# A fused retention and SwiGLU kernel: the first head pair by 128 tokens, and the loads of its start in another order

## The chip, the cores and the metric

The kernel runs on one core of a Trainium2 chip. A core has five engines that run at the same time, each through its own instructions in order: TensorE (matmuls; the profile shows weight loads apart from the streaming), VectorE, ScalarE, GpSimd and SyncE. SyncE and ScalarE also issue most of the DMA transfers here, and GpSimd a few. TensorE writes to PSUM, in eight banks; VectorE and ScalarE take results out of there into SBUF.

The metric is the time of one execution on the device, in microseconds (us). A profile of one execution is the source of everything that is said of single instructions.

## The reference

Two stages are fused: a retention (attention with a decay in place of the softmax), and a SwiGLU feed-forward block on its output.

```python
B, H, S, D = 8, 8, 576, 64            # q, k, v, float32
gamma = 1.0 - 2.0 ** (-5.0 - arange(H))
scores = (1 / sqrt(D)) * q @ k.T
ret = scores * where(i >= j, gamma ** (i - j), 0)
attn = ret @ v
x = attn.transpose(0, 2, 1, 3).reshape(4608, 512)
g, val = x @ w_gate, x @ w_val        # 512 x 1536 each, float64
out = (g * sigmoid(g) * val) @ w_out  # 1536 x 512, float64
```

The weights come as float64 and are turned into float32 on the chip.

## The kernel before

**Retention.** The work goes by pairs of heads: pair `i` holds heads `2p` and `2p + 1` of one batch entry, four pairs to an entry, 32 in all. The first four pairs (`i < HP`, HP = 4) make the first 512 tokens of `x`, the first tile; everything below concerns them. A pair is cut into chunks of 64 tokens. In a chunk the decayed scores times the values give its own part ("own values"); what comes from earlier chunks goes through a running state of 64 x 64 per head ("earlier values").

For one pair of the first four the steps are:

- `load(i)` (L254) asks for q, k and v. Pairs 0 and 1 are asked for on SyncE's and ScalarE's queues, one head on each, pairs 2 and 3 on SyncE's. A small table of decays, `tab`, comes first on SyncE's queue (L311); its rest, which the pairs after the first four use, comes between pairs 2 and 3 (L337).
- `scale_run(i)` (L730), GpSimd: the queries of pairs 1 to 3 are multiplied by their decay.
- `transposes(i)` (L448): four 128 x 128 transposes each of k and q on TensorE, copies of the two out of PSUM (`kT` and `qT`; ScalarE, and for pair 0 partly VectorE), and the keys scaled by decay (`keys`, on VectorE for pair 0, ScalarE for pair 1, GpSimd for 2 and 3).
- `scores(i)` and `new_states(i)` (L562, L537): 64 x 64 matmuls into the banks `inner`.
- `masked(i)` (L576): ScalarE copies the even chunks' states (`even`), VectorE multiplies the scores by the decay (`own`), then adds up the states (`pairs`, `odd`, three steps of 64 columns, and `evens`).
- `own_values(i)` and `earlier_values(i)` (L524, L546): 64 x 64 matmuls into the banks `outer`.
- `to_x(i)` (L613): the result goes to the tile of `x`, on VectorE for pair 0, on ScalarE for pairs 1 to 3.

A float32 matmul of the code stands as two records in the trace, a transpose as one: `scores(i)` has 16 matmuls and 32 records.

**Weights.** There are 18 blocks of 1 MB, each for 256 columns of the gate or value weights, or 256 rows of the output weights. `load_w(m)` (L359) asks for the m-th of them, up to `m = 4` on SyncE's queue and later ones on ScalarE's. It writes into one of a few places in turn, so it has to wait for the splits that read the block there before. A block has two halves (128 columns); `halves` numbers them j: 0 is the first half of the first gate block, 1 the first half of the first value block, 2 and 3 their second halves, 4 and 5 the halves of the second gate block, and so on. `split(j)` (L380) is two ScalarE instructions that take the float64 apart, `rounding(j)` (L399) two on VectorE that make the float32; `rounding(j)` also emits `split(j + 1)` unless told not to. `split(2)` emits `load_w(4)`, and `split(3)` puts `load_w(5)` off to a given place.

**Feed-forward of the first tile.** `up0(f, chunks)` (L842) multiplies columns `f` of the gate (into bankA or bankC) and of the value weights (into bankB or bankE) with the given pairs' parts of `x`, one 512-wide matmul for a pair and a weight. It takes banks A and B for even `f`, C and E for odd. When the last pair is in, ScalarE applies the SiLU and VectorE multiplies.

**Order.** From L1425 on each engine's instructions stand in the order in which the code emits them. L1427 to L1436 run the first four pairs: `tick(t, 0, HP)` (L737) has stage by stage one pair's transposes, the next older one's scores and states, and the next older one's values. In `tick(3)` and `tick(4)` the first splits, roundings and `up0(0, [0, 1])`, `up0(1, [0, 1])` stand between; after them come chunks 2 and 3 of both. `load(HP)`, the fifth pair, is issued after `tick(3)`. From L1444 a plan goes on with `up0(2)` to `up0(11)`, the roundings that each needs, and the ticks of pairs 4 to 9; `tick(HP)`, the transposes of pair 4, is its second entry. The tiles after the first (from L1511) take most of the time and are the same before and after.

Of the kernel before, what the change touches and what calls it, by code (L numbers as in the profile page):

```python
# [17 lines left out]
ALU = mybir.AluOpType  # L18
# [4 lines left out]
def tables(gamma, scale, L):  # L23
# [15 lines left out]
             both(g[:, None] ** L), both(g[:, None] ** (2 * L)), pieces, runs, both(scale * g[:, None] ** at),  # L39
# [92 lines left out]
def kernel(  # L132
# [32 lines left out]
    nc = tc.nc  # L165
# [88 lines left out]
    def load(i):  # L254
# [6 lines left out]
        if i < HP:  # L261
# [11 lines left out]
            for h in heads:  # L273
                queues[i % 2].dma_start(out=blocks(t)[:, h % 2], in_=v[b, h, 0:CW].rearrange("(c p) d -> p c d", p=P))
# [35 lines left out]
    NCOL = 6 * H + 4 * HP  # L310
    nc.sync.dma_start(out=tab[:, 0:NCOL], in_=decays[:, 0:NCOL])  # L311
    load(0)
    load(1)
    ident = const.tile([P, P], F32, name="ident")
    make_identity(nc, ident)
    nc.scalar.activation(out=io[:, 0:1], in_=ident[:, 0:1], func=AF.Silu)
    inv, key = tab[:, 0:H], tab[:, H : 2 * H]
    step = tab[:, 2 * H : 2 * H + 2 * HP]
    piece = tab[:, 2 * H + 2 * HP : 2 * H + 4 * HP]
    run = tab[:, 2 * H + 4 * HP : NCOL]  # L320
# [11 lines left out]
    even_heads, odd_heads = slice(0, H, 2), slice(1, H, 2)  # L332
    for rows in half:
        decay(slice(0, H), slice(0, H), rows)

    load(2)
    nc.sync.dma_start(out=tab[:, NCOL:], in_=decays[:, NCOL:])  # L337
    load(3)
# [20 lines left out]
    def load_w(m, parts=range(2)):  # L359

        i, queue = order[m], nc.sync if m < 5 else nc.scalar
# [49 lines left out]
    for f in range(2):  # L411
        for m in range(2):
            load_w(m, (f,))
# [30 lines left out]
    def vector(i):  # L444

        return i == 0

    def transposes(i):  # L448
# [6 lines left out]
        copy = nc.scalar.copy if i else nc.vector.tensor_copy  # L455
        if i < HP:

            mine = (bankC, bankE) if i + 1 == HP else (bankB, bankA)
            parts = [(kT, kn, mine[0]), (qT, qk, mine[1])]
            if i == 0:  # L460
                parts.reverse()

            def turn(t, src, bank):
                for c in range(NFULL):
                    to = bank[:, c : 4 * P : NFULL] if t is qT and scaled(i) else bank[:, ts(c, P)]
                    nc.tensor.transpose(to, src[:, ts(c, P)], ident)

            def put(t, _, bank):
                if i or t is qT:
                    copy(t[:, 0:CW], bank)  # L470
                else:
                    copy(t[:, 0 : CW // 2], bank[:, 0 : CW // 2])
                    nc.scalar.copy(t[:, CW // 2 : CW], bank[:, CW // 2 :])

            if i + 1 == HP:
                for part in parts:
                    turn(*part)
# [1092 lines left out]
```

## Time and profile before

| | |
|---|---|
| median of 3 runs | 1015.25 us (1015.02 to 1017.70) |
| the profiled execution | 1014.55 us, of which 1012.8 us is the span from first to last instruction |
| TensorE streaming | 1000.9 us, 99% of the span |
| TensorE loading weights | 825.5 us, beside the streaming |
| VectorE, ScalarE, GpSimd | 710.9, 286.7, 561.8 us |
| TensorE busy in the first 10 us, in 10 to 20, 20 to 30, 30 to 40 | 4.50, 9.03, 8.83, 9.82 us |
| TensorE busy from 40 to 100 us | 60.00 us |
| data moved in the first 60 us | 15.58 MB |

A view of the profile names an instruction by the line of the code (L532), the engine, the operation, and the tile it writes and reads; `rest` and `arena` are large areas of SBUF that hold many things in turn, `bankA` to `bankE`, `inner` and `outer` are PSUM. "PE" is TensorE, "PEld" its weight loads, "DVE" VectorE, "ACT" ScalarE, "POOL" GpSimd, "SP" SyncE; a q after the name is the engine's sequencer, which issues transfers. "x32" says that 32 such instructions are merged in a row. "[1.16 <-PE outer L559]" says that the engine was idle for 1.16 us before, and what ended that. Busy time of an engine that is not on the chain of waits costs nothing by itself.

### The profile page before, as it was taken

The numbers are of one execution on the slowest core, as the hardware profiler recorded it, in microseconds if no ns is written. First come the engines' busy times: TensorE is split into PE (matmuls) and PEld (weight loads), VectorE is DVE, ScalarE is ACT, GpSimd is POOL, SyncE is SP. The second block draws the span as 40 slices with busy tenths as digits, with TensorE's granted clock in tenths as the row PEclk, the third lists the DMA queues.
The fourth block names the chain that finished last, engine by engine and source line by source line (L and its number), as shares of the span: only waits on it lengthen the run. The fifth ranks groups of instructions, "written<-read, shape, count | busy, mean of one in ns | idle before, by whom it ended". The sixth has DMA issues, their size and how long they took to land.

```text
span 1012.8 us, 21319 instructions
## 1 busy us (share of the span) xinstructions
PE 1000.9 (99%) x8336; PEld 825.5 (82%) x8336; DVE 710.9 (70%) x1206; ACT 286.7 (28%) x636; POOL 561.8 (55%) x589
## 2 busy tenths in 40 slices
PE   6999999999999999999999999999999999999998
PEld 5655555888888888888888888888888888888887
DVE  4488887677875766977777678866575767566645
ACT  4565522132423312133422202233220012232110
POOL 3400359979375228575564157746672586566514
PEclk9999999999999999999999999999999999999999
DMA  9999866967587787647677777434454554445553
GB/s 245 261 288 272 192 216 234 264 193 214 138 238 207 217 231 193 198 156 196 184 202 206 198 179 217 154 133 159 161 172 141 154 189 147 148 155 180 182 159 102
DMA packets 278892, 194.38 MB, mean 192 GB/s; under 512 B 212552, under 2 KB 246088, under 8 KB 278792
## 3 DMA queue, kind: packets, MB, share of 16 engines
q1 hardware_dynamic: 251464, 94.70, 36.7%
q10 hardware_dynamic: 26688, 97.92, 29.1%
q8 instruction: 66, 1.08, 0.5%
q0 software_dynamic: 640, 0.39, 0.2%
q14 instruction: 34, 0.28, 0.1%
HBM read 154.04 MB, written 38.93 MB: 191 GB/s over the span
## 4 chain that ended last, share of the span: by engine, by line
PE 94%; DVE 2%; DMA 1%; POOL 1%; SPq 0%; issue 0%; ACT 0%; DVEq 0%; ACTq 0%; POOLq 0%
PE bankB L1186 12%; PE bankC L1186 11%; PE bankA L1186 11%; PE bankE L1186 11%; PE bankB L1392 7%; PE bankC L1392 7%; PE bankE L1392 6%; PE bankA L1392 6%; PE outer L532 2%; PE bankE L853 2%; PE bankA L853 2%; PE outer L1186 2%; PE inner L1186 2%; PE bankB L853 2%; PE outer L559 2%; PE bankC L853 2%
## 5 line engine op out<-in xcount | busy, mean ns | idle before, releaser
L1042 POOL TENSOR_TENSOR rest<-rest 128x512 f32<-128x512 f32 (+1 forms) x139 | 148.0, 1076 | 159.9 <-DVE rest L1042 112.5
L1201 POOL TENSOR_TENSOR arena<-rest,io 128x256 f32<-128x256 f32 x168 | 123.9, 750 | 89.4 <-ACT io L1200 88.9
L1200 ACT ACTIVATE io<-rest 128x256 f32<-128x256 f32 x192 | 79.3, 417 | 200.0 <-DVE rest L1042 140.0
L1186 PE MATMUL bankB<-rest,arena 128*128 128x256 f32 x448 | 114.5, 380 | 0.0
L1042 DVE TENSOR_TENSOR rest<-bankB,rest 128x512 f32<-128x512 f32 x116 | 78.5, 685 | 40.5 <-PE bankB L1186 28.5
L1186 PE MATMUL bankC<-rest,arena 128*128 128x256 f32 x416 | 106.3, 380 | 0.0
L1186 PE MATMUL bankA<-rest,arena 128*128 128x256 f32 x412 | 104.8, 379 | 0.0
L1042 DVE TENSOR_TENSOR rest<-bankA,rest 128x512 f32<-128x512 f32 x111 | 75.2, 685 | 40.8 <-PE bankA L1186 19.3
L1042 DVE TENSOR_TENSOR rest<-bankC,rest 128x512 f32<-128x512 f32 x110 | 74.5, 683 | 38.0 <-PE bankC L1186 23.4
L1042 DVE TENSOR_TENSOR rest<-bankE,rest 128x512 f32<-128x512 f32 x106 | 71.7, 684 | 36.2 <-PE bankE L1186 17.6
L1186 PE MATMUL bankE<-rest,arena 128*128 128x256 f32 x372 | 94.9, 380 | 0.3 <-DVE rest L1042 0.3
L1186 PEld LDWEIGHTS bankB<-rest,arena 128*128 128x128 f32 x448 | 84.7, 190 | 11.9 <-DVE rest L1042 0.2
L1186 PEld LDWEIGHTS bankC<-rest,arena 128*128 128x128 f32 x416 | 78.5, 190 | 11.4 <-DVE rest L1042 0.8
L1186 PEld LDWEIGHTS bankA<-rest,arena 128*128 128x128 f32 x412 | 78.1, 190 | 10.9 <-DVE rest L1042 0.2
L1186 PEld LDWEIGHTS bankE<-rest,arena 128*128 128x128 f32 x372 | 70.3, 190 | 10.4 <-DVE rest L1042 0.8
L1042 POOL TENSOR_TENSOR arena<-arena 128x256 f32<-128x256 f32 (+1 forms) x76 | 70.3, 947 | 11.1 <-PE bankC L1186 9.0
L886 POOL TENSOR_TENSOR rest<-rest 128x512 f32<-128x512 f32 x21 | 28.5, 1377 | 72.1 <-DVE rest L407 58.5
L1392 PE MATMUL bankB<-arena 128*128 128x256 f32 x264 | 61.0, 381 | 0.0
L1392 PE MATMUL bankE<-arena 128*128 128x256 f32 x264 | 60.8, 380 | 0.0
L1392 PEld LDWEIGHTS bankE<-arena 128*128 128x128 f32 x264 | 50.0, 190 | 6.9
L1392 PEld LDWEIGHTS bankB<-arena 128*128 128x128 f32 x264 | 49.8, 190 | 6.9
L1392 PE MATMUL bankC<-arena 128*128 128x256 f32 x240 | 55.2, 379 | 0.0
(270 smaller groups left out, 1876.0 us busy)
## 6 DMA issues: line engine op xcount, KB each, us to landing
arena<-up ACTq DMA_DIRECT2D x63, 896.0 KB, 4.6
arena<-dn ACTq DMA_DIRECT2D x65, 384.0 KB, 3.1
arena<-dn SPq DMA_DIRECT2D x39, 384.0 KB, 3.1
out_dram<-rest SPq DMA_DIRECT2D x31, 256.0 KB, 3.4
qk<-in_q_dram SPq DMA_DIRECT2D x108, 72.0 KB, 3.1
qk<-in_k_dram SPq DMA_DIRECT2D x108, 72.0 KB, 3.4
dn<-rest SPq DMA_DIRECT2D x26, 256.0 KB, 2.8
up<-arena SPq DMA_DIRECT2D x13, 512.0 KB, 5.6
```

Of the source, the lines that this page charges most:

```text
L532: m = nc.tensor.matmul(value(i, hl, c), s["v"][rows, at], ret[rows, c % 2 if whole(i) else hl, c // 2], start=start, stop=start, skip_grou ...
L559: nc.tensor.matmul(xr[half[hl]] if c + 1 == NC else value(i, hl, c), state[half[hl], c, :], s["qT"][half[hl], ts(c, L)], start=False, stop ...
L853: nc.tensor.matmul(bank, w, xs[0][:, c, :], start=(c == 0), stop=(c == HP - 1))
L886: eng.tensor_tensor(out=dst, in0=srcs[0], in1=srcs[1], op=ALU.add if op[0] == "add" else ALU.subtract)
L1042: eng.tensor_tensor(out=out, in0=a, in1=b, op=ALU.add if sign > 0 else ALU.subtract)
L1186: m = nc.tensor.matmul(b[:, g * TB : (g + 1) * TB], w[:, g], x, start=(opens and g == 0), stop=True, skip_group_check=True)
L1200: nc.scalar.activation(out=s, in_=src[:, 0:TB], func=AF.Silu)
L1201: (nc.vector if busy and o != 2 and qd + 1 < NQ else nc.gpsimd).tensor_tensor(out=hid[:, qd, 2 * H + h, 2 * T + t], in0=src[:, TB : 2 * TB ...
L1392: nc.tensor.matmul(b[:, m * TB : (m + 1) * TB], lhs[:, qd, ts(m, P)], w[:, qd], start=(opens and qd == 0 and m == 0), stop=(qd == NQ - 1), ...
```

## The change

The first pair gets code of its own. Its tokens are taken by 128: scores are four blocks of 128 x 128 for each head, there are three state steps in place of seven, and the decay is in its queries already, by a table of their own, so that its result is copied to `x` by ScalarE. Matmuls of the identity, whose result nobody reads, stand ahead of and between its transposes. The table `tab` starts with three more pieces (132 columns) for it.

The loads: the table comes after the first k on SyncE's queue; the values of pairs 0 and 1 are asked for after the queries and keys of both; the first half of the first gate block comes ahead of pair 2, the first half of the first value block ahead of pair 3; `load_w(5)` moves from ScalarE's queue to SyncE's, and both it and `load_w(4)` stand ahead of the fifth pair; the rest of `tab` comes after the fifth pair.

The ticks of the first four pairs are written out as a list in which `up0(0, ...)` is cut into four pieces, and `tick(HP)` is moved from the plan's second entry to just behind `up0(2)`.

```diff
-            for h in heads:
-                queues[i % 2].dma_start(out=blocks(t)[:, h % 2], in_=v[...])
+                if i == 0 and queue is nc.sync:
+                    nc.sync.dma_start(out=tab[:, 0:NCOL], in_=decays[:, 0:NCOL])
+            def values():
+                for h in heads:
+                    queues[i % 2].dma_start(out=blocks(t)[:, h % 2], in_=v[...])
+            loaded[i] = (qk, kn, t)
+            return values
...
-    NCOL = 6 * H + 4 * HP
-    nc.sync.dma_start(out=tab[:, 0:NCOL], in_=decays[:, 0:NCOL])
-    load(0)
-    load(1)
+    NCOL = 6 * H + 4 * HP + 4 + P
+    values = [load(0), load(1)]
     ident = const.tile([P, P], F32, name="ident")
     make_identity(nc, ident)
     nc.scalar.activation(out=io[:, 0:1], in_=ident[:, 0:1], func=AF.Silu)
+    for f in values:
+        f()
...
-    load(2)
-    nc.sync.dma_start(out=tab[:, NCOL:], in_=decays[:, NCOL:])
-    load(3)
...
-        i, queue = order[m], nc.sync if m < 5 else nc.scalar
+        i, queue = order[m], nc.sync if m < 6 else nc.scalar
...
-    for f in range(2):
-        for m in range(2):
-            load_w(m, (f,))
+    load_w(0, (0,))
+    load(2)()
+    load_w(1, (0,))
+    load(3)()
+    for m in range(2):
+        load_w(m, (1,))
     load_w(2)
     load_w(3)
...
+    def first_scores():
...
+        for _ in range(10):
+            nc.tensor.matmul(bankB[:, 0:32], ident, ident[:, 0:32], start=True, stop=True)
+        for src, bank, idle in ((None, None, 4), (qk, bankE, 2), (kn, bankC, 1)):
+            for c in range(NFULL if bank else 0):
+                nc.tensor.transpose(bank[:, ts(c, P)], src[:, ts(c, P)], ident)
+            for _ in range(idle):
+                nc.tensor.matmul(bankB[:, 0:P], ident, ident, start=True, stop=True)
+        nc.vector.tensor_tensor(out=blocks(qT), in0=blocks(bankE), in1=table(first_qry), op=ALU.mult)
+        nc.vector.tensor_copy(kT[:, 0 : CW // 2], bankC[:, 0 : CW // 2])
+        nc.scalar.copy(kT[:, CW // 2 : CW], bankC[:, CW // 2 :])
+        for hl in range(2):
...
+            nc.vector.tensor_scalar(out=at, in0=at, scalar1=first_key[:, hl : hl + 1], scalar2=None, op0=ALU.mult)
+        for c, hl in first:
+            nc.tensor.matmul(inner[:, hl, ts(c, P)], kT[half[hl], ts(c, P)], qT[half[hl], ts(c, P)], ...)
+        for hl in range(2):
+            nc.vector.tensor_tensor(out=first_ret[:, hl], in0=blocks(inner[:, hl]), in1=table(first_near[:, ts(hl, P)]), op=ALU.mult)
+    def first_states():
+        for c, hl in first:
+            nc.tensor.matmul(sums[half[hl], c], s["kn"][:, head(c, hl)], s["v"][:, head(c, hl)], ...)
+        nc.vector.tensor_copy(state[:, 1], sums[:, 0])
+        for c in range(1, NFULL):
+            nc.vector.scalar_tensor_tensor(out=..., in0=state[:, c], scalar=step[:, HP : HP + 1], in1=sums[:, c], ...)
+    def first_own():
+        for c, hl in first:
+            nc.tensor.matmul(outer[half[hl], 0, ts(c, P)], st[0]["v"][:, head(c, hl)], first_ret[:, hl, c], ...)
+    def first_out():
...
+        for c, hl in first[2:]:
+            nc.tensor.matmul(outer[half[hl], 0, ts(c, P)], state[half[hl], c], s["qT"][half[hl], ts(c, P)], ...)
+        nc.scalar.copy(out=xs[0][:, 0], in_=outer[:, 0])
+    def new_pair(i):
+        scores(i, True)
+        new_states(i)
+        pieces.extend(masked(i))
+        go_on(3)
+    def turn_pair(i):
+        for f in transposes(i):
+            f()
...
-    for t in range(HP + 2):
-        tick(t, 0, HP)
-        if t == 3:
-            load(HP)
-        for j in {3: (1,), 5: (4, 5)}.get(t, ()):
-            rounding(j)
+    scale_run(1)
+    first_scores()
+    scale_run(2)
+    turn_pair(1)
+    first_states()
+    first_own()
+    new_pair(1)
+    first_out()
+    split(0)
+    rounding(0, False)
+    own_values(1)
+    up0(0, [0], [0])
+    earlier_values(1)
+    turn_pair(2)
+    to_x(1)[0]()
+    split(1)
+    scale_run(3)
+    new_pair(2)
+    put = transposes(3)
+    rounding(1, False)
+    for f in put:
+        f()
+    up0(0, [1], [0])
+    up0(0, [0], [1])
+    split(2)
+    own_values(2)
+    earlier_values(2)
+    up0(0, [1], [1])
+    to_x(2)[0]()
+    rounding(2)
+    rounding(3, False)
+    new_pair(3)
+    while held:
+        held.pop()()
+    load(HP)
+    nc.sync.dma_start(out=tab[:, NCOL:], in_=decays[:, NCOL:])
+    split(4)
+    up0(1, range(2))
+    own_values(3)
+    earlier_values(3)
+    to_x(3)[0]()
+    for j in (4, 5):
+        rounding(j)
...
-    plan.insert(1, lambda: tick(HP, HP, FIRST))
     tick_at = {2: 4, 3: 5, 5: 6, 7: 7, 10: 8, 11: 9}
     for f in range(2, NF):
+        if f == 3:
+            plan.append(lambda: tick(HP, HP, FIRST))
```

In `up0(f, chunks, parts)` the new `parts` picks the gate weights (0) or the value weights (1). For the first four pairs `transposes` now always uses bankC and bankE and returns its copies ahead of its scaled keys.

## The prediction

> **What bounds the kernel now.** I read the page first, then the busy time by windows, the chain of waits in order of time, and the timeline of the first 60 us.
>
> ```profile
> span 1012.8 us, 21319 instructions
> ...
> PE 1000.9 (99%) x8336; PEld 825.5 (82%) x8336; DVE 710.9 (70%) x1206; ACT 286.7 (28%) x636; POOL 561.8 (55%) x589
> ...
> PE 94%; DVE 2%; DMA 1%; POOL 1%; SPq 0%; issue 0%; ACT 0%; DVEq 0%; ACTq 0%; POOLq 0%
> ```
> TensorE is the bound. Where does it idle? The windows (us, length, busy time and records of each engine, clock, DMA share, GB/s) say: only in the head.
>
> ```profile
> 0.00:40.00 40.00, 32.19 (x558) 21.63 (x559) 20.08 (x44) 19.62 (x39) 17.43 (x33) 1.00 1.06 252
> 40.00:100.00 60.00, 60.00 (x536) 34.18 (x535) 45.53 (x99) 34.52 (x62) 4.22 (x8) 1.00 1.06 275
> 100.00:200.00 100.00, 99.91 (x1013) 61.77 (x1013) 78.23 (x131) 33.10 (x79) 69.55 (x67) 1.00 0.78 226
> ```
> All that the diff touches lies there, so the change is worth the shift of one anchor, the first matmul of `up0(2)` (L850), after which TensorE waits for nothing. The chain up to it (start, us, what):
>
> ```profile
> 1.74 4.14 DMA kn<-in_k_dram
> ...
> 5.89 3.73 DMA kn<-in_k_dram
> ...
> 13.49 0.85 PE inner L543 x32
> ...
> 16.24 0.85 PE bankA L466 x4
> 17.09 0.69 PE outer L559 x28
> ...
> 21.20 0.45 PE bankE L466 x4
> ```
> Two keys loads end first; then four transposes take 0.85 at 16.24 but 0.45 at 21.20, and 32 records of 64x64 take 0.85 at 13.49 where later rows have 0.53 to 0.74. So TensorE runs at half speed until about 17 (the profile's clock row says 1.00 throughout, so the durations decide), and is let go between 3.9 and 4.7 us after its last gap, from 12.36 to 16.24 or 17.02. The rows from which ScalarE and VectorE are priced, and the anchor:
>
> ```profile
> 20.66 1.13 ACT L640 COPY rest<-outer 128x256 f32<-128x256 f32 x3 [1.16 <-PE outer L559]
> ...
> 22.82 0.67 ACT L389 ACTIVATE rest<-rest 128x512 f32<-128x512 f32 x1
> ...
> 23.39 0.69 ACT L390 ACTIVATE rest<-rest 128x512 int32<-128x512 uint32 x1
> ...
> 27.74 0.56 PEld L573 LDWEIGHTS inner<-rest,kT 64*64 64x64 f32 x32 [0.76 <-ACT rest L640]
> ...
> 40.95 3.62 PE L850 MATMUL bankA<-rest,arena 128*128 128x256 f32 x16
> ```
>
> **Method and prices.** I lay the instructions on their engines in program order, each starting when its engine is free and its operands are there. Prices, start to start. ScalarE: copy of kT or qT 0.59, of `even` 0.37, keys of pair 1 0.96, `to_x` 1.13, a split 1.13 (two records 0.57 apart). VectorE: multiply of 512 0.60 (result after 0.69), pairs 0.50, three 64-wide steps 1.0, evens 0.47, one rounding 1.2 (0.42, 0.69 and the gap). GpSimd: run scaling 1.04, keys 1.9. TensorE at full speed: four transposes 0.45, scores 0.57, states 0.55, own 0.62, earlier 0.60, a 512-wide matmul 0.86 (two records of 0.43). Laid out so, the order of before reaches the anchor at 40.8; the trace shows 40.95. The method holds to 0.2 us.
>
> **Part 1, the warm-up matmuls (added).** Ten of 32 columns and four of 128 precede the transposes of q, two and one follow. Each is two records, and each record loads 128 weight columns. The nearest row is a transpose, which also loads 128: 0.213 at half speed (0.85 / 4). I take that for both widths: 28 records are 6.0 us from 1.55 (identity done: 1.21 + 0.29). If the clock is let go 4.7 us after 1.55, at 6.2, the last six cost 0.107 (0.43 x 128/512) and the block ends at 6.9. Bounds: if only the columns that stream count, the 32-wide record costs 0.053 and the block ends near 4.4; if loads don't overlap (0.19 a record at full speed, 0.34 at half), near 9. For the clock the rows give 5.4 at the earliest (3.9 us) and, counted from the scores at 7.62, where the first longer stretch begins, 9.4 us or 10.9 at the latest. The queries are no longer waited for: they land at 4.6 now and are asked for 0.4 earlier.
>
> The Trainium skill ("TensorE: Matmul & The Clock Gate", LDWEIGHTS) says that a weight load takes as long as its columns whatever is streamed; by it a 32-wide warm-up saves nothing over a 128-wide one, which is the value taken above. The same page (Part 1) frees the clock after one fully busy window of 3.4 us that runs freely, so between 5.0 and 8.4 here; the 3.9 to 4.7 us of the trace agree. By its two ends the anchor of the ladder below would be 42.1 and 43.8.
>
> **Part 2, the first pair by 128 tokens.** Removed: its 32 score, 32 state, 32 own and 28 earlier records (0.57 + 0.55 + 0.62 + 0.60 = 2.34 at full speed) and VectorE's 1.29 of `to_x`. Added on TensorE: 16 score records of 128 columns on half the rows, 16 of 64, 16 of 128, 12 of 128. By columns, alone: 1.71 + 0.86 + 1.71 + 1.28 = 5.56; two at a time on the halves of the array: 2.78. The trace has no such shape; it has 64x64 records going four at a time (32 in 0.85 at half speed, where 64 columns alone are 0.107), so I take two at a time. VectorE has 0.69 + 0.42 + 0.62 + two multiplies 1.2 + copy 0.15 + three steps 0.95 = 4.0 for 0.69 + 0.42 + 0.62 + 0.6 + 0.5 + 1.0 + 0.47 + 1.29 = 5.6; ScalarE's 0.59 copy to x replaces `even`, 0.37. GpSimd gets one more select (about 0.5), hidden: it ends near 7, ahead of pair 1's run scaling.
>
> **Part 3, the loads of the head.** SyncE's order becomes q, k, the table (100 KB for 32), pair 1's q and k, values of pair 0, first gate half, pair 2, first value half, pair 3, the rest; ScalarE asks for the values of pair 1 behind its table load (1.28). Before, 1.0 MB had moved by 6 us, 1.7 by 9, 2.5 by 12, 3.3 by 15, 4.2 by 18 (DMA view). Up to pair 1's keys 1.1 MB are asked, the gate half 2.2, pair 2 2.9, the value half 3.5, pair 3 4.2: with some 0.5 us to the semaphore they land near 7 (9.6 before), 11, 13, 16 and 18.5. The ladder needs them at 9.9, 14.8, 18.8, 21.8 and 22.0: 3 to 6 us of cover each. An issue takes SyncE 0.34 to 0.50 us, so the seven ahead of the weights are out by 4, as fast as the data. With every arrival 1 to 2 us later the ladder doesn't move.
>
> **Part 4, the ladder.** Transposes of q at 6.94, two idle matmuls, of k at 7.82; half the copy (0.42), scores at 9.0 (7.6 before). Transposes of pair 1 9.9 to 10.8; the two multiplies end 11.35; sums and own values follow; scores of pair 1 at 12.26 (12.36 before). So the early keys pay for the warm-up and no more. ScalarE's copies and keys of pair 1 end 12.7, its states 13.5, `even` 14.0, VectorE's evens 16.0, `rounding(0)` 17.3. Here is the first new wait: `up0(0, [0], [0])` stands ahead of `earlier_values(1)` and needs `rounding(0)`, which stands behind the evens on VectorE. TensorE, free at 15.6, goes on at 17.36. Transposes of pair 2 start at 18.8 (15.1 before, but own and earlier values of pair 1 and one piece, 2.1 us, are then done that came later).
> ScalarE: kT, qT, `to_x(1)`, `split(1)` from 19.5 to 22.9, and only then `even` of pair 2, 23.3. VectorE: pairs, steps, evens to 25.4, `rounding(1)` 26.6. Second new wait: the value piece `up0(0, [0], [1])` stands ahead of `own_values(2)` and needs `rounding(1)`; TensorE, free at 23.8, goes on at 26.63. Own, earlier, a piece; scores of pair 3 at 29.7 (27.8 before). From there the order is that of before, 13.0 us: anchor at 42.7, **1.75 us later**.
>
> **Part 5, what is moved behind the head.** `load_w(5)` goes from ScalarE's queue (29.6) to SyncE's and waits there for `split(3)`, done near 31.3 to 32.8; with the 5.6 us from issue to landing it is there by 39 and needed near 58: free. Behind it queue pair 4 (its issues took 28.0 to 38.8), the rest of the table, pair 5. Pair 4 then lands near 46 to 51, and `tick(HP)` is moved behind `up0(2)`, to about 50 on VectorE; its results are needed at 56.5 (anchor + 13.8). Cover 3 us with 1.5 of stream transposes; if it is gone, TensorE loses what is missing, one for one.
>
> **Sum.** 1014.55 (profiled time; span 1012.8) + 1.75 = 1016.3; the median of the runs is 0.7 higher, so **1017.0**.
>
> **The rivals.**
> (a) *The clock stays at half speed* (slower). The place is the first pair: 32-wide streams leave the array mostly empty, and in the trace 4 us of transposes and 64x64 records (7.62 to 11.65) did not free it. A release at 9.0 puts the anchor at 44.2 and is where the loss passes 3 us; at 10.9, the late bound, the pair's scores, pair 1's transposes and the own values run at half speed too and it is 45.5, +4.6: 1019.9. Against it: there is no gap now as at 11.65. On the same page (Part 4) transposes don't count as activity, which speaks for this rival only where they fill the window.
> (b) *No two at a time* in the 128-token matmuls: 2.78 more in the pair, of which 2.6 reach the anchor: 45.3, +4.4, 1019.6. For it: no row of this shape. Against: the 64x64 rows.
> (c) *Short warm-up*: 32-wide records cost their columns, so q is transposed by 4.4: anchor 40.4 (clock free at 5.4, 128-wide ones at 0.213 a matmul) to 41.5 (6.2): -0.5 to +0.5, 1014.7 to 1015.8, no change.
> (d) *The waits for the roundings don't form* (faster). TensorE's own work from 6.9 to the anchor is 27.9, so 7.9 of the ladder is waiting. All gone would be 34.8, -6.1: 1009.1; half of it 1013.0. For it: the weights land 6 us ahead of their splits. Against: VectorE and ScalarE kept program order in every row that I compared.
> (e) *Pair 4 comes too late* behind the two weights: +3 and more, 1019.
>
> **How the numbers follow.** Forecast 0.40, with its own range 1016.8 to 1018.5 from a release between 5.4 (anchor 42.5) and 9.0; (a) 0.15, (b) 0.12, (c) 0.15, (d) 0.13, (e) 0.05. 0.3% is 3.05 us, about what a measurement of this kernel can tell. Faster: (d), 0.13. Within: 0.35 of the forecast and (c), 0.50. Slower: 0.05 of the forecast's upper end, (a), (b) and (e), 0.37. The range leaves out most of (d) below and the worst of (a), (b) above: 1013.0 to 1020.2.
>
> **What would show it.** First transposes of q near 6.9, not near 4.5; scores of pair 1 near 12.3; records of pair 0 at 0.107 per 128 columns from about 6 on; an idle TensorE ahead of the first and the third piece of `up0(0)`, released by the second record of a rounding; the anchor near 42.7. An anchor below 40 would refute the ladder, and any wait of TensorE between 45 and 110 the claim that the rest is only shifted.

## The result and the profile after

The changed kernel is slower: 1025.3 us in the median of 6 runs (1023.18 to 1027.97) against 1016.5 for the kernel before on the same chip, a ratio of 1.0089 (95% interval 1.0073 to 1.0105). The profiled execution took 1023.76 us with a span of 1022.1, so 9.3 us more span than before. The forecast was 1017.0 us, with a range up to 1020.2.

First where the time went. These are the windows of the changed kernel (us from the start, length, busy time and records of TensorE, its weight loads, VectorE, ScalarE, GpSimd; then the clock, the DMA share and GB/s):

```profile
0.00:10.00 10.00, 8.45 (x42) 8.45 (x42) 0.69 (x1) 1.49 (x2) 3.56 (x12) 1.00 0.96 202
10.00:20.00 10.00, 6.85 (x168) 5.80 (x167) 6.66 (x17) 4.34 (x9) 1.04 (x1) 0.98 1.09 233
20.00:30.00 10.00, 7.20 (x112) 4.38 (x110) 2.67 (x7) 5.70 (x12) 4.67 (x5) 0.85 1.02 285
30.00:40.00 10.00, 8.98 (x177) 4.89 (x181) 6.26 (x13) 3.79 (x8) 2.86 (x6) 1.00 0.74 235
...
100.00:150.00 50.00, 48.86 (x636) 25.52 (x635) 41.38 (x86) 25.14 (x54) 13.68 (x10) 1.00 0.91 223
```
TensorE now idles for 3.1 us from 10 to 20 and for 2.8 from 20 to 30, where it had 9.03 and 8.83 us of work before. The clock column drops to 0.85 at the same place, and 1.1 us are lost again beyond 100 us, where nothing was lost before. TensorE's timeline of the head (start, us, what; in brackets the idle time before and what ended it):

```profile
1.55 4.47 PE L732 MATMUL bankB<-ident 128*128 128x32 f32 x20 [1.55 <-POOL ident masks.py:199]
...
7.68 1.06 PE L735 MATMUL bankE<-ident,qk 128*128 128x128 f32 x4
...
9.39 0.62 PE L735 MATMUL bankC<-ident,kn 128*128 128x128 f32 x4
...
14.17 0.69 PE L558 MATMUL inner<-rest,kT 64*64 64x64 f32 x32
...
19.54 1.98 PE L869 MATMUL bankA<-rest,arena 128*128 128x512 f32 x2 [2.13 <-DVE arena L415]
21.45 1.12 PE L544 MATMUL outer<-rest 64*64 64x64 f32 x28
22.51 0.91 PE L466 MATMUL bankC<-ident,rest 128*128 128x128 f32 x4
...
26.96 1.02 PE L869 MATMUL bankA<-rest,arena 128*128 128x512 f32 x2
...
30.75 1.13 PE L869 MATMUL bankB<-rest,arena 128*128 128x512 f32 x2 [2.77 <-DVE arena L415]
...
34.26 0.69 PE L558 MATMUL inner<-rest,kT 64*64 64x64 f32 x32
...
47.44 3.62 PE L866 MATMUL bankA<-rest,arena 128*128 128x256 f32 x16
```
Both new waits stand where the prediction put them: ahead of the first gate piece and ahead of the first value piece of `up0(0)`, each ended by VectorE's second rounding record (L415). But the two 512-wide records of that first piece take 1.98 us where two take 1.02 elsewhere (26.96 and later). So TensorE is at half speed again, after it had been let go near 9.4 (four transposes 1.06 at 7.68, 0.62 at 9.39). The anchor, the first matmul of `up0(2)` (now L866), is at 47.44, 6.5 us later than the 40.95 of before. The other 2.8 of the 9.3 come behind it: 1.1 is a wait in `down0`, the output matmuls of the first tile, 0.9 are two waits that the profile gives to nothing (L1408), and the rest is spread. The executions of the kernel before lie between 1014.2 and 1020.1 us in its largest group of 28 runs, so 2.8 us between two profiles are weak evidence; the 6.5 us of the anchor can be followed row by row.

VectorE's and ScalarE's rows ahead of the second wait show how it forms:

```profile
24.47 1.15 ACT L625 COPY rest<-outer 128x256 f32<-128x256 f32 x3
...
26.79 0.37 ACT L569 COPY even<-inner 128x256 f32<-128x256 f32 x1
```
```profile
27.20 0.69 DVE L565 TENSOR_TENSOR ret<-inner,near 128x512 f32<-128x512 f32 x1 [7.71 <-ACT even L569]
...
29.16 0.48 DVE L593 SCALAR_TENSOR_TENSOR state<-state,tab,even 128x256 f32<-128x256 f32 x1
...
30.00 0.69 DVE L415 CUSTOM_DVE_ANT_0 arena<-arena,rest 128x1024 uint16<-128x1024 uint16 x1
```
VectorE's multiply of pair 2 doesn't start when its scores are there but when ScalarE's copy of `even` ends (27.16), though it does not read `even`: both read the banks `inner`, and the program puts the two readers in order. The same row follows the same copy in the kernel before; the prediction's ladder had no such edge. The multiply takes 0.60 us before the next step can start (27.80), so the edge is a small part of the delay. Most of it is handed on: the transposes of pair 2 are late (22.51), so ScalarE takes up the pair at 23.51 and comes to `even` behind `to_x(1)` (L625) and `split(1)` only at 26.79.

Behind the anchor, these are the lines of the chain of waits and of ScalarE's timeline:

```profile
71.66 11.06 DMA v<-in_v_dram
...
91.22 10.80 DMA kn<-in_k_dram
...
107.06 8.11 DMA rest<-in_moe_w_out_dram
...
132.27 1.12 PE bankE L880 x2
```
```profile
102.05 0.96 ACT L492 ACTIVATE kn<-kn,tab 128x256 f32<-128x256 f32 x2 [5.60 <-DMA kn<-in_k_dram]
```
The later pairs' keys and values are on the chain now, and ScalarE, which has splits and SiLUs queued behind the scaling of the keys (L492), stands 5.60 us for one pair's keys. Just ahead of the wait in `down0` two records of VectorE are slow, 1.49 and 1.54 us in place of 0.42 and 0.69; they are so in the kernel before, too (120.56 and 122.19), where TensorE does not wait. SyncE's timeline, after and then before, shows why the keys are late:

```profile
29.28 0.37 SPq L378 DMA_DIRECT2D rest<-in_moe_w_gate_dram  x1
35.64 0.37 SPq L378 DMA_DIRECT2D rest<-in_moe_w_val_dram  x1
36.10 3.59 SPq L290 DMA_DIRECT2D qk<-in_q_dram  x4
...
49.76 2.01 SPq L290 DMA_DIRECT2D qk<-in_q_dram  x4
```
```profile
27.95 4.07 SPq L282 DMA_DIRECT2D qk<-in_q_dram  x4
...
42.14 4.67 SPq L282 DMA_DIRECT2D qk<-in_q_dram  x4
```
The sixth block waits for its split on SyncE from 29.65 to 35.64. The fifth pair behind it is asked for at 36.10 in place of 27.95, the sixth pair at 49.76 in place of 42.14.

### The profile page after: what moved, and what is told of

Read it like the earlier page. It is cut to its first block, busy times and chain, and to the rows that moved or that the text cites. A ratio compares the mean times of both kernels' runs of the same rounds, so it can differ in the third digit from the quotient of the medians.

```text
span 1022.1 us, 21256 instructions
## 1 busy us (share of the span) xinstructions
PE 1007.5 (99%) x8306; PEld 830.7 (81%) x8306; DVE 710.8 (70%) x1203; ACT 286.0 (28%) x636; POOL 561.4 (55%) x590
## 4 chain that ended last, share of the span: by engine, by line
PE 89%; DMA 4%; DVE 3%; ACT 1%; SPq 1%; issue 1%; ACTq 0%; DVEq 0%
PE bankB L1202 12%; PE bankC L1202 12%; PE bankA L1202 11%; PE bankE L1202 11%; PE bankB L1408 7%; PE bankE L1408 7%; PE bankC L1408 7%; PE bankA L1408 6%; PE inner L1202 2%; PE outer L1202 2%; PE outer L517 2%; DMA v<-in_v_dram 2%; PE outer L544 1%; PE inner L558 1%; PE inner L528 1%; DMA kn<-in_k_dram 1%
## 5 line engine op out<-in xcount | busy, mean ns | idle before, releaser
L902 POOL TENSOR_TENSOR rest<-rest 128x512 f32<-128x512 f32 x21 | 29.0, 1401 | 77.5 <-DVE rest L415 59.9
L1408 PE MATMUL bankB<-arena 128*128 128x256 f32 x264 | 61.2, 381 | 0.7 <-issue 0.7
L1408 PE MATMUL bankE<-arena 128*128 128x256 f32 x264 | 60.8, 380 | 0.0
L1408 PEld LDWEIGHTS bankB<-arena 128*128 128x128 f32 x264 | 49.8, 190 | 7.8 <-issue 0.9
L1408 PEld LDWEIGHTS bankE<-arena 128*128 128x128 f32 x264 | 50.0, 190 | 6.9
L1408 PE MATMUL bankC<-arena 128*128 128x256 f32 x240 | 55.2, 379 | 0.0
```

Source lines behind the costliest of these rows:

```text
L902: eng.tensor_tensor(out=dst, in0=srcs[0], in1=srcs[1], op=ALU.add if op[0] == "add" else ALU.subtract)
L1408: nc.tensor.matmul(b[:, m * TB : (m + 1) * TB], lhs[:, qd, ts(m, P)], w[:, qd], start=(opens and qd == 0 and m == 0), stop=(qd == NQ - 1), ...
```

## The experiments

The numbers of one profiled execution are set side by side here; "behind" is the span less the anchor. The ratios are against the kernel before on the same chip.

| kernel | anchor | behind | median | ratio (95%) |
|---|---|---|---|---|
| before | 40.95 | 971.9 | 1015.5 to 1016.5, one for each group of runs | 1 |
| after | 47.44 | 974.7 | 1025.3 | 1.0089 (1.0073 to 1.0105) |
| e1_nowarm | 46.79 | 982.9 | 1031.6 | 1.0150 (1.0135 to 1.0165) |
| e2_later | 42.50 | 975.5 | 1020.4 | 1.0045 (1.0030 to 1.0061) |
| e3_ownfirst | 48.91 | 975.6 | 1026.3 (one run) | |
| e4_loadsback | 49.20 | 972.3 | 1025.5 | 1.0089 (1.0067 to 1.0111) |
| e6_both | 42.77 | 972.3 | 1018.9 | 1.0033 (1.0020 to 1.0046) |
| e7_both_warm7 | 39.92 | 988.3 | 1024.3 | 1.0085 (1.0055 to 1.0114) |
| e8_bef_loads | 41.62 | 972.0 | 1016.3 | 1.0002 (0.9990 to 1.0015) |
| e9_bef_warm | 40.87 | 972.0 | 1015.8 | 1.0001 (0.9988 to 1.0014) |
| e10_later_warm7 | 40.21 | 980.7 | 1022.5 | 1.0064 (1.0050 to 1.0077) |
| e11_beforder | 40.16 | 980.4 | 1021.8 | 1.0063 (1.0051 to 1.0075) |
| e12_beforder_tab | 43.06 | 982.0 | 1024.9 | 1.0091 (1.0073 to 1.0109) |
| e13_both_warm7_tab | 41.84 | 980.7 | 1024.4 | 1.0087 (1.0067 to 1.0106) |
| e14_later_tab | 42.80 | 978.4 | 1022.9 | 1.0064 (1.0049 to 1.0078) |
| e15_both_tab | 42.14 | 977.4 | 1020.1 | 1.0027 (1.0011 to 1.0043) |

The runs of these kernels spread by 0.9 to 9.5 us, and a profile is one of them: e6_both's (1016.8) is its fastest of 12, e7_both_warm7's (1029.9) the slowest of 6. So the ratios say what is faster, the rows only how.

**e1_nowarm: the changed kernel without its identity matmuls.**

```diff
-        for _ in range(10):
-            nc.tensor.matmul(bankB[:, 0:32], ident, ident[:, 0:32], start=True, stop=True)
-        for src, bank, idle in ((None, None, 4), (qk, bankE, 2), (kn, bankC, 1)):
+        for src, bank, idle in ((None, None, 0), (qk, bankE, 0), (kn, bankC, 0)):
```


> The changed kernel without its 17 identity matmuls. Theory W (the warm-up block costs the loss): the queries are transposed at 4.3 to 4.6 in place of 7.5 and the anchor (first matmul of up0(2)) comes 3 us earlier than 47.4. Theory O (the loss sits in the order of the pieces behind the roundings): TensorE is then at half speed until 14 to 17, scores of pair 1 come at about 14.6 (14.2 now), and the anchor stays between 46 and 48; the time is within 1.5 us of the changed kernel's.

The transposes of q start at 4.08 in place of 7.68, and the scores of pair 1 at 13.86 in place of 14.17: the clock was let go only at 13.6, so the warm-up had bought back what it had delayed, no more. The anchor comes 0.65 earlier and the whole kernel is slower still, by a loss behind the anchor that stays open (4.6 us of it are one wait, from 95.0, that the profile gives to nothing). The warm-up is not what makes the head late.

**e2_later: the two pieces that had the new waits, one stage later.**

```diff
     own_values(1)
-    up0(0, [0], [0])
     earlier_values(1)
     turn_pair(2)
+    up0(0, [0], [0])
...
     up0(0, [1], [0])
-    up0(0, [0], [1])
     split(2)
     own_values(2)
     earlier_values(2)
+    up0(0, [0], [1])
```


> The changed kernel with up0(0,[0],[0]) moved behind turn_pair(2) and up0(0,[0],[1]) behind earlier_values(2); all else as it is. Theory O: TensorE no longer waits for rounding(0) ahead of the earlier values of pair 1, so it neither idles 2 us there nor falls back to half speed; transposes of pair 2 near 18.8 (22.5 now), the anchor at 42 to 43, 4 to 5 us earlier than 47.4, and the time 4 to 5 us shorter. Theory W: no change of the anchor by more than 1 us, since the first pair is as late as before.

TensorE's timeline of e2_later:

```profile
18.80 0.68 PE L544 MATMUL outer<-rest 64*64 64x64 f32 x28 [0.96 <-DVE rest L593]
19.42 0.66 PE L466 MATMUL bankC<-ident,rest 128*128 128x128 f32 x4
...
20.35 1.02 PE L869 MATMUL bankA<-rest,arena 128*128 128x512 f32 x2
...
27.41 1.98 PE L869 MATMUL bankB<-rest,arena 128*128 128x512 f32 x4 [0.39 <-DVE arena L415]
```
The first piece has its rounding when TensorE comes to it, and the value piece waits 0.39 us in place of 2.77. Transposes of pair 2 start at 19.42 in place of 22.51, at full speed (the clock reads 1.00 in every window of this execution). The anchor is 4.9 us earlier and the median 4.9 us lower; the two intervals don't touch. Shown: about half of the loss is the place of these two pieces (0.0044 of 0.0089 by the ratios). What it leaves in the head is 1.55 us; behind the anchor nothing is mended in this execution, and TensorE waits 1.7 us in `down0`.

**e3_ownfirst: VectorE's multiply emitted ahead of the copy of `even`.**

```diff
-        return [copies, own, [pairs, odd, evens] if i < HP else [last, pairs, odd, evens]]
+        return [own, copies, [pairs, odd, evens]] if i < HP else [copies, own, [last, pairs, odd, evens]]
```


> The changed kernel with VectorE's score multiply emitted ahead of ScalarE's copy of the even states for the first pairs. If the multiply waits for the copy only because the program puts the two readers of the bank in order, it now starts right behind the states' matmuls and the copy waits for it instead: pair 2's multiply near 26.2 in place of 27.2, and the copy behind it. If it is the hardware that holds the two readers apart by who is ready, the order stays as it is. The anchor moves by less than 1 us either way, since the sums still need both.

The order of the two readers turns round and no more: the multiply starts at 26.61, ended by TensorE's states, and now the copy waits for it and runs at 27.39.

```profile
26.61 0.69 DVE L565 TENSOR_TENSOR ret<-inner,near 128x512 f32<-128x512 f32 x1 [6.66 <-PE inner L528]
27.79 0.48 DVE L581 SCALAR_TENSOR_TENSOR state<-even,tab,inner 128x256 f32<-128x256 f32 x1 [0.49 <-ACT even L569]
```
The next step (L581) needs both, and comes at 27.79; in the changed kernel it comes at 27.80, with scores that were 0.45 us earlier. So the missing edge is worth some 0.45 us of this pair's states (and nothing at pair 1, where the copy now comes later), and not the anchor: that got 1.5 us later, where 1 at most was expected, with the first pieces at half speed again (two records 1.79 at 20.00, 2.07 at 30.84).

**e4_loadsback: the later loads where the kernel before has them.**

```diff
-        i, queue = order[m], nc.sync if m < 6 else nc.scalar
+        i, queue = order[m], nc.sync if m < 5 else nc.scalar
...
+    load(HP)
+    nc.sync.dma_start(out=tab[:, NCOL:], in_=decays[:, NCOL:])
     split(2)
...
     round_until(3)
+    plan.insert(1, lambda: tick(HP, HP, FIRST))
```
(The same lines are taken out where the change had put them.)

> The changed kernel with load_w(5) on ScalarE's queue again, the fifth pair asked for ahead of split(2) and its transposes back at the plan's second entry (the rest of the table goes with the fifth pair). Theory L (the loads moved behind the head cost the part of the loss that comes after the anchor): the anchor stays near 47.4, but TensorE's wait of 1.1 us in down0 near 131 is gone and the time is 1 to 3 us shorter. Rival: the wait in down0 comes from the head's shift alone and stays; the time is within 1 us.

The wait in `down0` is gone, and the time behind the anchor is 972.3, 0.4 from that of before. But in this execution the clock fell to half a second time, from 31.0 to 34.5, the anchor came 1.8 later, and the median is that of the changed kernel. That the order of the loads makes the wait in `down0` is not shown: e3_ownfirst has the changed loads and no such wait, e11_beforder (below) has them back and waits 2.2 us there.

**e6_both: e2_later and e4_loadsback together.**

> The changed kernel with both orders mended: the two gate pieces of the first feed-forward column behind the next pair's work (as in e2_later) and the fifth pair's loads, the sixth weight block and the fifth pair's transposes put back to where the kernel before has them (as in e4_loadsback). Theory (two separate losses, the order in the head and the order of the loads): the first matmul of up0(2) near 42.5 us as in e2_later, no wait of TensorE in down0 as in e4_loadsback, so e2_later's span of 1018.0 less its wait of 1.7: about 1016.3, and a ratio of about 1.002. Rival (the loads only change places, and an early fifth pair delays the third and fourth halves of the weights): a wait of more than 1 us ahead of the second value piece, up0(2) at 44 us or later, a ratio of 1.004 or more.

The anchor is at 42.77, there is no wait in `down0`, and the span of the profiled run is 1015.1: the theory's rows. The ratio is between the two, 1.0033; its interval overlaps e2_later's, so a gain of the load order by itself is not shown in the times. In this execution, the fastest of its twelve, most of what is left (1.8 of 2.3 us) lies in the head.

**e8_bef_loads and e9_bef_warm: one part of the change in the kernel before.** In e8_bef_loads the sixth block is on SyncE's queue and the fifth pair and its transposes stand behind (the edits as in the change); e9_bef_warm has this:

```diff
+    for _ in range(7):
+        nc.tensor.matmul(bankC[:, 0:32], ident, ident[:, 0:32], start=True, stop=True)
     for t in range(HP + 2):
         tick(t, 0, HP)
...
                     put(*part)
+                    for _ in range(2 if i == 0 else 0):
+                        nc.tensor.matmul(bankC[:, 0:P], ident, ident, start=True, stop=True)
```


> The kernel before with the load moves alone: the sixth weight block on SyncE's queue, the fifth pair asked for behind it, its transposes behind up0(2); the rest of the table stays where it was. Theory (this order of loads costs something after the head, by itself): up0(2) still at 40.9 to 41.2, a wait of TensorE of 1 to 2 us in down0 near 125 us or in the 50 us behind it, and 1016 to 1017.5 in all, a ratio of 1.001 to 1.002. Rival (the loads cost nothing where the head isn't late): no wait of TensorE between 41 and 150, a ratio within 0.001 of 1.

> The kernel before with a warm-up alone: seven 32-column matmuls of the identity ahead of its first transposes and two of 128 columns behind each four. Theory (the clock is released by busy time, so the first 17 us of the kernel before are at half speed without need): transposes of pair 1 near 9.7 take 0.43 for four in place of 0.85, scores of pair 1 near 11.5 in place of 12.4, up0(2) 0.5 to 1.7 earlier than 40.95, a ratio of 0.9985 to 0.9995. Rival (the head of the kernel before is held by copies, splits and roundings, ahead of its own values at 22.62 by ScalarE): up0(2) within 0.3 of 40.95 and a ratio of 1.

Both rivals held: neither part alone moves the time (1.0002 and 1.0001). In e8_bef_loads ScalarE waits for keys four times from 40 to 130 us, 15.2 us in all (9.6 in the changed kernel), and TensorE doesn't wait: there late keys cost nothing by themselves. In e9_bef_warm the clock is free from 9.0 us on (17.1 before), transposes of pair 1 take 0.60 to 0.66 for 1.06 to 1.12, and the anchor comes 0.08 earlier: the head of before is held by the copies, splits and roundings, as the rival has it, not by TensorE's speed.

**e7_both_warm7, e10_later_warm7, e11_beforder: heads that are early.** The first two shorten the warm-up of e6_both and e2_later to 7 matmuls ahead of the transposes and one after each four; e11_beforder has the first pair by 128 tokens and that warm-up in the stage order and with the later loads of the kernel before, but the table's rest behind the fifth pair.

> As e6_both, with a shorter warm-up: seven 32-column matmuls of the identity and none of 128 ahead of the first transposes, one behind each four (14 + 4 records in place of 28 + 6). Theory (the warm-up is longer than the clock needs, since the queries land near 4.6 us): transposes of q near 4.7, of k near 6.0, the first scores near 7.5, all at half speed, the clock full near 9 to 10, scores of pair 1 near 12.5 in place of 14.2 to 14.6, up0(2) near 41, a span 1.0 to 1.7 us under that of e6_both. Rival (the clock counts busy time, and gaps between the parts of the first pair set it back as in e1_nowarm): half speed until about 13, scores of pair 1 near 13.9, up0(2) not more than 0.6 earlier than in e6_both, or later.

> As e2_later (the two gate pieces behind the next pair's work; the loads in the changed order: the fourth and fifth gate and value blocks ahead of the fifth pair), with the short warm-up of e7_both_warm7. It differs from e7_both_warm7 in the order of the loads alone. Theory (with a head that is done early the weights bind: in e7_both_warm7 the second gate block of 1 MB was asked for at 45.73 us, behind the fifth pair, landed at 53.4 and kept TensorE waiting for 3.0 us; asked for ahead of the pair it is there): up0(2) near 39.9, that gate block asked for near 28 and landed near 36, no wait for SiLU near 55; the fifth pair lands near 50, so a wait of at most 1 to 2 us shows in or ahead of its transposes; 1014 to 1017, a ratio of 0.999 to 1.002. Rival (the loads together are the bound, 15.6 MB in 60 us, and whatever is asked first, the last of them is late): the wait moves to the fifth pair or to down0 and is 3 us or more, a ratio of 1.004 to 1.010 as in e7_both_warm7.

> The first pair by 128 tokens and the short warm-up, but everything else where the kernel before has it: the order of the first four pairs' stages, of the splits, roundings and feed-forward pieces, and the order of the loads (the table behind the first k, the values behind both pairs' q and k and the table's rest behind the fifth pair stay as changed). Against e9_bef_warm (64 tokens, up0(2) at 40.87) it shows what the first pair's new form is worth alone. Theory (the new form of the first pair neither costs nor gains much, since the order after it is set by splits and roundings): up0(2) between 39.9 and 41.2 and a ratio of 0.998 to 1.001. Rival (the new form itself costs, by its longer records and its copy on ScalarE): up0(2) at 41.5 or later and a ratio of 1.0015 or more.

All three bring the anchor ahead of the kernel before, to 39.9 to 40.2, and all three are 0.6 to 0.9% slower. In e11_beforder the anchor came as the theory had it and the ratio as the rival had it. What they win in the head they lose behind it. ScalarE's rows of e7_both_warm7 and TensorE's row behind them,

```profile
53.49 0.67 ACT L397 ACTIVATE rest<-rest 128x512 f32<-128x512 f32 x1 [5.23 <-DMA rest<-in_moe_w_gate_dram]
...
57.44 0.58 ACT L872 ACTIVATE io<-bankA 128x512 f32<-128x512 f32 x1
```
```profile
58.08 6.65 PE L869 MATMUL bankA<-rest,arena 128*128 128x512 f32 x8 [3.01 <-ACT io L872]
```
show a part of it. The fifth block (`load_w(4)`, the third of the gate; the expectations call it the second) was asked for at 45.73, and at 38.86 in the kernel before. Its split waits for its data, the SiLU that frees bankA stands behind that split on ScalarE, and TensorE waits 3.01 us (and runs its next eight records at half speed, 6.65 for 3.60). Before, the same split started at 49.29, the SiLU at 53.26, and TensorE came to bankA at 56.03, 2.2 us behind the SiLU's end. This is some 6 of the 16.4 us that this execution loses behind the anchor; 5.6 more are two waits that the profile gives to nothing. In e10_later_warm7, where the block is early, the keys are late instead (ScalarE waits 5.67 us for those of the fifth pair and 5.4 to 7.0 for the next three), and TensorE waits 2.2 for a SiLU at 102.7. In e11_beforder TensorE waits 3.0 for SiLUs and 2.2 in `down0`. The theory of e10_later_warm7 fell; the rows fit its rival, by which whatever is asked first, another load is late.

**e12_beforder_tab, e13_both_warm7_tab, e14_later_tab, e15_both_tab: the table's rest asked for early again**, between pair 2 and what follows it, in the heads of e11_beforder, e7_both_warm7, e2_later and e6_both.

> As e11_beforder, with one load moved: the rest of the table is asked for between pairs 2 and 3, where the kernel before has it, and no longer behind the fifth pair and ahead of the second gate block. What is left of the change is the first pair by 128 tokens, a short warm-up, and the order of pairs 0 and 1's own loads. Theory (the table's rest, 4.16 us of SyncE's issuing at 40.46 in e11_beforder, makes the gate block behind it late; it was asked for at 44.72, and at 38.86 in the kernel before): the gate block is asked for near 39 to 41, no wait of TensorE for SiLU near 55, up0(2) near 40.2, a span of 1011.5 to 1013, a ratio of 0.997 to 1.000. Rival (the head is now ahead of the loads, whatever their order, since up0(2) is 0.8 earlier than in the kernel before and the gate block landed there 2.2 before it bound): a wait of 1 us or more for SiLU or in down0, a ratio of 1.001 to 1.005.

> As e7_both_warm7 (the changed kernel's own order of the first pairs with the two gate pieces later, a short warm-up, the fifth pair's loads as before), with the rest of the table asked for between pair 2 and the first half of the first value block. Theory (the table's rest ahead of the gate block is what cost e7_both_warm7 its wait of 3.0 us): no such wait, up0(2) near 40, a span of 1011 to 1014 and a ratio of 0.997 to 1.001. Rival (the loads are late anyway, or the wait that the profile calls issue is what costs): a ratio of 1.004 or more, with a wait of 2 us or more between 50 and 140 us.

> As e2_later, with the rest of the table asked for between pair 2 and the first half of the first value block; the fourth and fifth gate and value blocks stay ahead of the fifth pair. Theory (the table's rest behind the fifth pair is what costs behind the head, since with it early, in e8_bef_loads, the two blocks cost nothing): no wait in down0 or one under 0.5 us, 1.5 to 3 us less than e2_later, a ratio of 1.001 to 1.003. Rival (the two blocks ahead of the fifth pair cost it, by putting every later pair's keys back, on which ScalarE waits ahead of its splits): the wait in down0 stays at 1 to 2 us, a ratio of 1.004 to 1.006.

> As e6_both, with the rest of the table asked for between pair 2 and the first half of the first value block. Theory (the table's rest costs): the second gate block is asked for 1 to 2 us earlier, the span is 0.3 to 1.5 us below e6_both's, a ratio of 1.001 to 1.0025. Rival (it costs nothing, or the value half that is now behind it comes late in the head): up0(2) at 42.8 or later and a ratio of 1.003 or more.

None is faster than its partner. The medians of e12 and e14 are higher than those of e11_beforder and e2_later, but the intervals of their ratios overlap. In e14_later_tab the wait in `down0` is gone, as its theory had it, and the time did not fall. So the place of the table's rest is not what makes these kernels slow. The later anchor of e13_both_warm7_tab, 41.84 for 39.92, is no measure of the table either: its clock was let go only at 13.4 us, and at 9.4 in e7_both_warm7. In e12_beforder_tab, where the fifth block is asked for at 41.25, ScalarE stands 5.94 us (35.25 to 41.19) at its issue of the seventh block, which waits for an earlier transfer of the fifth pair; the SiLU that `up0(2)` needs stands behind, and TensorE waits 3.06 for it. By the profile's releaser it is the fifth pair's loads once more, at another place.

No version beat the kernel before.

## Why the prediction was wrong

**What bounds, and the anchor.** That all loss would be a shift of the anchor was half right: it shifted by 6.5, not 1.75, and 2.8 were lost behind it in the profiled run. Part 5 gave the sixth block's move to SyncE as "free", and followed the queue behind it only to the fifth pair. It did foresee the wait for `split(3)`. It left out that every later pair is then asked for later too, and that ScalarE has splits and SiLUs queued behind the keys' scaling. How much of the 2.8 this cost is not shown: in e8_bef_loads the same moves of the sixth block and the fifth pair cost nothing. Rival (e) fell: TensorE has no wait from the anchor to 131. The refutation that the prediction had set itself, a wait between 45 and 110, therefore did not show.

**The step that failed: Part 4, the ladder.** Its places were right: both new waits, what releases them, and the last stretch, which was given 13.0 us from the scores of pair 3 to the anchor and took 13.18. Its times were not, and they go wrong in three steps.
- The clock. The ladder let it go at 6.2; it went at about 9.4, 7.9 us after the first matmul. The late end of Part 1's bounds (9.0, anchor 44.2), where rival (a) begins, is what happened. The scores of pair 1 were 1.9 late.
- The clock again. The ladder ran TensorE at full speed from then on. It fell back to half at the first new wait, until about 23; the first piece, the earlier values and the transposes behind took 1.7 us more than at full speed (0.96, 0.46 and 0.3). No part and no rival had this: rival (a) kept the clock low from the start.
- The readers of `inner`. In the ladder the multiply ran beside the copy of `even`; it has to follow it. This is the smallest of the three. `rounding(1)` ended at 30.69 in place of 26.6, and the second wait with it, but 3.7 of these 4.1 us were there when the transposes of pair 2 started (22.51 for 18.8).

Of the 4.7 us by which the anchor missed the ladder, 1.9 were there at the scores of pair 1, 0.3 more at the end of `rounding(0)`, 1.5 more at the transposes of pair 2, 0.4 more at the end of `rounding(1)`, and 0.6 came behind it.

The method "holds to 0.2 us" on the kernel before, but this was no test of its clock: e9_bef_warm shows that TensorE's speed is worth 0.08 there. A ladder that fits one order is not tested for another.

**Part 2** was nearly right: 16 records of 64 x 128 took 1.09 us where one after the other would be 1.71, so they overlap, if not quite two at a time (0.86); the four groups of the pair took 3.45 in all, where Part 2 had 2.78 and one after the other would be 5.56. Rival (b) fell. **Part 1**'s price was right too: 28 records of the block took 6.1 us at 0.22 (6.0 at 0.213), and rival (c) fell. **Rival (d)** fell: both waits formed. With the pieces moved (e2_later) they shrink, and 4.9 us come back.

The Trainium skill ("PSUM — Partial Sum Buffer", PSUM bank collisions raise a hardware error) says that the compiler's scheduler orders any two instructions on different engines that touch one bank and quadrant, reads against reads included. The rows agree (27.16 to 27.20 in the changed kernel, and the reversed order in e3_ownfirst); whoever holds it against the ladder finds the missing edge.

The Trainium skill ("TensorE: Matmul & The Clock Gate", Part 1) lets the clock go after about 3.4 us of activity and takes it back after an idle window as long. Here it went 7.9 us after the first matmul, and fell back at a gap of 2.13 us with another of 0.72 shortly ahead. In e6_both it fell back at 19.1 behind gaps of 0.72 and 0.96 alone. The measurements decide: gaps shorter than that window were enough.

**The clock's steps.** e2_later has the gaps of e6_both and kept its clock in the profiled run. The granted clock of all these traces changes only at whole steps of 3.41 us after its release. In the changed kernel it is let go at 9.43, falls three steps later, at 19.67, and returns at 23.08 (over windows cut at these times the clock column reads 1.00, then 0.50, then 1.00); in e6_both the three times are 8.89, 19.13 and 22.54. In e6_both both gaps lie in the step that ends with the fall, and TensorE is idle for 1.69 us of it (2.59 in the changed kernel). In e2_later, let go at 10.54, one gap lies in the step up to 17.37 and the other in the step behind it, and the clock stays. Where the steps lie against the program differs from execution to execution, so the fall in a given one is in part luck: the mean clock of the changed kernel is 0.995 to 0.998 in all six, that of e2_later 1.000 in seven of ten and 0.998 in three.

**What stays open.** How much idle time in a step is enough is not settled: e8_bef_loads fell behind 1.56 us, e7_both_warm7 and e10_later_warm7 kept the clock with 1.68. About half of the loss of the changed kernel is tied to the two pieces; the other half is not tied to any one part of the change. Why the first 40 us bring less data in some heads (in the mean 238 GB/s in e13_both_warm7_tab, from 201, 257, 284 and 211 in four windows of 10 us, and 252 before, from 203, 269, 287 and 247) was not found. Nor were waits of 1.7 to 4.6 us in e1_nowarm, e7_both_warm7 and the kernels from e10_later_warm7 to e14_later_tab that the profile gives to nothing ("issue", on the scores, L557 to L559).

## What to carry to other kernels

Before a piece is moved ahead of older work in an engine's order, ask whether the instruction that feeds it is already done there, not only whether it could be: here two pieces pulled forward by a stage cost about half of the 9 us. In a hand-made schedule count the edges between readers of one bank, and allow for the clock falling back at each new gap. And three heads that were done early gained nothing here: look for what lands last behind a head before shortening it.

## What the runs showed of the hardware

- TensorE's clock came and went within the first 35 us of the same program: let go between 8.5 and 10.6 us with a warm-up from 1.55 on (in e13_both_warm7_tab only at 13.4), at 13.6 without one (e1_nowarm, first matmul at 4.08), and half speed again for 3.41 or 6.83 us behind gaps of 0.7 to 3.1 us. The durations of equal records show it (two 512-wide ones 1.02 or 1.98); the clock column shows the falls, and reads 1.00 before the release.
- Matmuls that use half of the array's rows (64 x 128) overlapped: the 16 of the scores took 1.09 us (10.53 to 11.62), where one after the other would be 1.71 (16 of 0.107).
- Ahead of the wait in `down0`, VectorE's roundings took 1.49 and 1.54 us in place of 0.42 and 0.69, while GpSimd was busy with its own multiplies (L902) from 125.29 to 132.74. In the kernel before they took the same, beside GpSimd's from 118.76 to 126.09.
